# First loads of a linear-attention block kernel moved between two DMA queues and cut smaller, with three filler matmuls and a split last store

## The chip, the cores and the metric

The kernel runs on one core of a Trainium2 chip. The metric is device time in microseconds; lower is better. Executions of one kernel mostly agree within 0.3%. A profile is one execution taken by the hardware profiler; its times count from the start of its span, which is about 1.26 us shorter than the device time. Engines are PE (TensorE matmul), PEld (its weight loads), DVE (VectorE), ACT (ScalarE), POOL and SP. SP and ACT also issue DMA transfers: "sync queue" is SP's, "scalar queue" ACT's. All runs gave a correct result.

## The reference, cut to what matters

```python
x  = A_x                                   # (1, 2048, 448), bf16
xn = _layernorm(x)
s  = linear_attention(xn, A_wqkv, A_wo)    # 16 heads of 28, phi(t) = (t>0 ? t+1 : exp(t)) + 1e-6
h  = relu(xn @ B_w1 + B_b1) ** 2           # 448 -> 1792
g  = silu(h @ B_w2 + B_b2)
return x + s * g
```

## The kernel before

A small program object collects operations with their reads and writes. A list scheduler orders ACT, DVE and POOL from modelled times; PE and SP keep program order. The 2048 tokens are 16 tiles of 128. The head normalizes tiles 0 to 3 on DVE and ACT, transposes them on PE, and starts the k projection (k0, k1) and the first hidden units (H0 to H3).

The loads, in the order in which each queue issues them:

```python
load_x(0, 1)                               # tile 0, sync
load_x(1, 2, "act").prio = -118            # tile 1, scalar queue
load_k("sp", w_qkv, A_wqkv, "wk", 384, 2 * D)   # 384 rows in one transfer, then two 64-row tails
load_x(2, 4, "act").prio = -117            # tiles 2, 3, scalar queue
dma("act", b1r[0:NF, :], ...).prio = -115  # b1, scalar queue
load_w1("w1a", 0, 512, 2)                  # two 384-row parts, then two 64-row tails
load_x(4, 8)                               # tiles 4 to 7, 448 KB
load_w1("w1b", 512, 1024)
load_k("sp", w_qkv, A_wqkv, "wq", 0, 384)
load_w1("w1c", 1024, F)
# ... (later loads cut)
```

The head on PE, and what follows it on DVE:

```python
warm(10, wide=True)                        # ten 512-column fillers on a constant
# ...
turn(0, 0, "act")                          # two transposes of tile 0, evicted by ACT
turn(0, 1, "act")
turn(1, 0, "act")
mains(k0, (0, 1), [("xT", 0, 0)] + wnames("wk")[:1])
turn(1, 1, "dve")
mains(k0, (2,), [("xT", 0, 1)])
k_mains(k1, 1)
# ... (H0 to H3, tiles 2 and 3 cut)
rests(k0, k1)
k0.out()       # phi: exp on ACT, then two operations on DVE that free the PSUM bank
k1.out()
```

The scheduler put the statistics of tiles 4 and 5 on DVE ahead of the phi operations of k0 and k1. DVE works in this order, so a late tile 4 holds up phi, phi holds PSUM banks, and PE's fourth group of products (H4, H6) needs those banks.

The last tile is stored once, after both column parts are done:

```python
full(ss(15, ca, eng="dve", end=False), KS, ["msz"])
full(gg(15, cb, True), range(NF + 1))
full(ss(15, cb, eng="dve", end=False), KS, ["msz"])
store(15, [ca, cb], "act")
```

## Time and profile before

| | before |
|---|---|
| device time, first 3 runs | 142.25 us median (142.16 to 142.40) |
| span of the profiled run | 141.2 us |
| first transpose, first k matmul on PE | 5.26, 6.16 us |
| tiles 4 to 7: issued, landed, used by DVE | 5.31, 9.23, 10.07 us |
| last store: issued, landed | 139.45, 141.17 us |

The page of the kernel before, busy microseconds with their share of the span, and from its part on the chain that ended last the shares by engine:

```profile
PE 137.8 (98%) x1225; PEld 68.4 (48%) x1225; DVE 92.0 (65%) x224; ACT 78.7 (56%) x152; POOL 22.9 (16%) x38
...
PE 98%; DVE 0%; issue 0%; DVEq 0%
```

PE is the limit nearly everywhere. A time lost on PE anywhere is lost at the end, and a wait elsewhere costs nothing until PE waits for it.

The timeline of DVE of the kernel before (start, duration, engine, line, operation, output and inputs):

```profile
9.73 0.42 DVE L513 COPY xT<-pb 128x512 bf16<-128x512 bf16 x1 [0.32 <-PE pb L503]
10.07 1.14 DVE L451 BATCH_NORM_STATS2 st<-x_tok 128x6 f32<-128x448 bf16 x2
11.13 0.67 DVE L595 TENSOR_SCALAR qk<-qk 128x512 bf16<-128x512 bf16 x2
11.71 1.28 DVE L602 SCALAR_TENSOR_TENSOR qk<-pb,qk 128x512 bf16<-128x512 f32 x2
```

The statistics of tiles 4 and 5 (10.07 us) stand ahead of the phi of k (11.13 and 11.71 us), and start without a wait: their data has been there for 0.84 us (10.07 - 9.23).

The table by stage of the kernel before: stretch in us, busy time and number of instructions of PE, PEld, DVE, ACT, POOL, then the granted PE clock, the mean busy share of the 16 DMA engines, and GB/s:

```profile
3.00:4.00 1.00, 1.00 (x4) 0.37 (x3) 0.60 (x1) 0.00 (x0) 0.64 (x3) 1.00 0.95 311
...
8.00:9.00 1.00, 1.00 (x13) 0.79 (x11) 0.85 (x4) 0.65 (x3) 0.00 (x0) 1.00 1.00 366
...
12.00:14.00 2.00, 2.00 (x22) 0.91 (x20) 2.00 (x6) 1.97 (x6) 0.00 (x0) 1.00 0.69 241
```

The DMA engines move over 300 GB/s from 3 to 4 and from 8 to 9 us, and PE is busy for all of the stretch from 12 to 14 us.

The end of the kernel before, from the timeline:

```profile
139.16 0.26 DVE L973 TENSOR_TENSOR xn<-xn,x_tok 128x192 bf16<-128x192 bf16 x1
139.45 0.37 ACTq L396 DMA_DIRECT2D out_dram<-xn  x1
```

The landing records of this store end at 141.17 us: it takes 1.72 us from issue to landing.

### The profile page before, as it was taken

The page shows a single profiled execution, that of the slowest core. Times are in us where ns is not written, and L with a number is a line of the kernel's source. Part 1 is how long each engine was busy: PE and PEld are TensorE (multiplying, and loading weights), DVE is VectorE, ACT ScalarE, POOL GpSimd, SP SyncE. Part 2 cuts the span into 40 slices and gives each one's busy share as a digit, 9 for nine tenths or more (in the row PEclk, how much of TensorE's full clock was granted, in tenths as well). Part 3 has the DMA queues.
Part 4 walks back from the last instruction along what each step waited for, and adds up shares of the span by engine and source line. Part 5 has one row for each costly group of instructions (what it writes and reads, how often), then busy time and mean ns, then how long its engine had stood idle before and what let it go on. Part 6 is the DMA issues. An engine that isn't in the chain of part 4 may idle for free.

```text
span 141.2 us, 3056 instructions
## 1 busy us (share of the span) xinstructions
PE 137.8 (98%) x1225; PEld 68.4 (48%) x1225; DVE 92.0 (65%) x224; ACT 78.7 (56%) x152; POOL 22.9 (16%) x38
## 2 busy tenths in 40 slices
PE   7999999999999999999999999999999999999992
PEld 2366444444444444444445445654555555555482
DVE  0989978898878998779959910127936062452743
ACT  3558787987888897879799571333033030300220
POOL 6000000000000000000680000000001419092670
DMA  4997266999713400000000025880000202122032
GB/s 111 310 312 235 50 170 97 366 300 210 137 23 74 84 14 0 0 9 14 0 0 0 5 76 151 200 155 14 5 0 0 68 2 89 41 66 69 33 102 67
DMA packets 20210, 12.91 MB, mean 91 GB/s; under 512 B 9380, under 2 KB 19812, under 8 KB 20196
## 3 DMA queue, kind: packets, MB, share of 16 engines
q1 hardware_dynamic: 18044, 11.22, 32.1%
q10 hardware_dynamic: 2152, 1.50, 4.4%
q8 instruction: 10, 0.16, 0.5%
q14 instruction: 4, 0.03, 0.1%
HBM read 8.78 MB, written 2.10 MB: 77 GB/s over the span
## 4 chain that ended last, share of the span: by engine, by line
PE 98%; DVE 0%; issue 0%; DVEq 0%
PE pb L928 30%; PE pb L661 30%; PE pb L614 9%; PE pb L994 8%; PE pb L695 7%; PE pb L645 6%; PE pb L1035 3%; PE pb L503 1%; PE pb L701 1%; PE pb L788 1%; PE pb L749 1%; PE pb L826 0%; DVE xn L964 0%; PE pb L819 0%; DVE xn L973 0%; PE pb L784 0%
## 5 line engine op out<-in xcount | busy, mean ns | idle before, releaser
L661 PE MATMUL pb<-xT,w 64*128 64x512 bf16 (+2 forms) x408 | 51.3, 365 | 0.0
L928 PE MATMUL pb<-w,r 64*128 64x448 bf16 (+3 forms) x378 | 44.7, 343 | 0.0
L670 ACT ACTIVATE r<-pb,b1f 128x512 bf16<-128x512 f32 x56 | 35.0, 690 | 2.8 <-PE pb L661 2.8
L661 PEld LDWEIGHTS pb<-xT,w 64*128 64x128 bf16 (+1 forms) x408 | 22.8, 94 | 22.1 <-ACT r L670 0.5
L928 PEld LDWEIGHTS pb<-w,r 64*128 64x128 bf16 (+1 forms) x378 | 22.8, 95 | 20.0 <-issue 1.2
L904 ACT ACTIVATE gbuf<-gbuf 128x448 bf16<-128x448 bf16 (+1 forms) x16 | 8.6, 564 | 36.4 <-DVE gbuf L939 34.3
L939 DVE TENSOR_TENSOR gbuf<-pb,b2b 128x448 bf16<-128x448 f32 (+1 forms) x16 | 9.3, 608 | 29.3 <-PE pb L928 29.3
L973 POOL TENSOR_TENSOR xn<-xn,x_tok 128x448 bf16<-128x448 bf16 x15 | 15.0, 1030 | 48.8 <-DVE xn L964 48.8
L614 PE MATMUL pb<-w_qkv,xT 64*128 64x512 bf16 (+1 forms) x106 | 17.9, 379 | 0.0
L645 PE MATMUL pb<-xT,w_qkv 64*128 64x512 bf16 x84 | 15.5, 376 | 0.0
L678 DVE TENSOR_TENSOR r<-r 128x512 bf16<-128x512 bf16 x39 | 13.5, 416 | 0.0
L385 POOL MEMSET kvm<- 128x2048 bf16 x1 | 1.8, 1804 | 64.4 <-DVE zb L639 64.4
L451 DVE BATCH_NORM_STATS2 st<-x_tok 128x6 f32<-128x448 bf16 x16 | 9.3, 611 | 3.4 <-DMA x_tok<-in_A_x_dram 3.4
L592 ACT ACTIVATE qk<-pb 128x512 bf16<-128x512 f32 x16 | 8.9, 594 | 4.1 <-PE pb L614 3.6
L602 DVE SCALAR_TENSOR_TENSOR qk<-pb,qk 128x512 bf16<-128x512 f32 x16 | 10.7, 686 | 0.3
L994 PE MATMUL pb<-msb,pqT 64*128 64x448 bf16 (+3 forms) x93 | 10.9, 343 | 0.0
L964 DVE TENSOR_TENSOR xn<-pb,gbuf 128x448 bf16<-128x448 f32 (+2 forms) x17 | 9.2, 590 | 2.0 <-ACT gbuf L904 1.5
L679 ACT ACTIVATE r<-r 128x512 bf16<-128x512 bf16 x17 | 9.7, 651 | 0.0
L614 PEld LDWEIGHTS pb<-w_qkv,xT 64*128 64x128 bf16 (+1 forms) x106 | 6.7, 95 | 6.2 <-DVE xT L513 0.2
L695 PE MATMUL pb<-qk,xn 128*128 128x448 bf16 x48 | 9.4, 352 | 0.0
L592 ACT ACTIVATE pqT<-pb 128x512 bf16<-128x512 f32 x12 | 6.8, 597 | 3.1 <-PE pb L661 1.6
L645 PEld LDWEIGHTS pb<-xT,w_qkv 64*128 64x128 bf16 x84 | 6.0, 94 | 5.0
(77 smaller groups left out, 98.9 us busy)
## 6 DMA issues: line engine op xcount, KB each, us to landing
out_dram<-xn SPq DMA_DIRECT2D x15, 112.0 KB, 1.7
w<-in_B_w_dram SPq DMA_DIRECT2D x1, 1568.0 KB, 9.8
x_tok<-in_A_x_dram SPq DMA_DIRECT2D x3, 448.0 KB, 3.8
xT<-rows ACTq DMA_DIRECT2D x6, 112.0 KB
w<-in_B_w_dram SPq DMA_DIRECT2D x1, 576.0 KB, 5.7
xT<-rows SPq DMA_DIRECT2D x5, 112.0 KB
w_o<-in_A_wo_dram SPq DMA_DIRECT2D x1, 392.0 KB, 11.0
w_qkv<-in_A_wqkv_dram SPq DMA_DIRECT2D x1, 384.0 KB, 4.7
```

The lines of the kernel that those rows point to most:

```text
L592: add("act", lambda e, _: e.activation(out=slot, in_=src(), func=AF.Exp), [buf, "actw"], [tile], 0.6)
L602: lambda e, _: e.scalar_tensor_tensor(out=slot, in0=src(), scalar=1.0 + 1e-6, in1=slot, op0=ALU.add, op1=ALU.max),
L614: return e.matmul(ps(b)[:, 0:512], xT[half[h], c, si * P : (si + 1) * P], w_qkv[half[h], c, 384 : 2 * D], start=start, stop=stop,)
L645: return e.matmul(ps(b)[:, 0:512], w_qkv[half[h], c, m * P : (m + 1) * P], xT[half[h], c, g * 512 : (g + 1) * 512], start=start, stop=stop,)
L661: return e.matmul(ps(b)[:, c0 : c0 + n], w_1[half[h], c, fi * P : (fi + 1) * P], xT[half[h], c, t : t + n], start=start, stop=stop,)
L670: lambda e, _: e.activation(out=slot, in_=ps(b)[:, 0:512], func=AF.Relu, bias=b1f[:, fi : fi + 1]),
L678: return e.tensor_tensor(out=slot, in0=slot, in1=slot, op=ALU.mult)
L679: return e.activation(out=slot, in_=slot, func=AF.Square)
L695: last = e.matmul(ps(b)[:, 0:D], xn[:, si, c * P : (c + 1) * P], pk_of(si), start=(si == 0), stop=(si == NT - 1),)
L928: return e.matmul(ps(b)[:, 0:n], r2[half[h], fi, si * P : (si + 1) * P], w_2[half[h], fi, c], start=start, stop=stop)
L973: eng, lambda e, _: e.tensor_tensor(out=ob, in0=ob, in1=x_tok[:, si, c], op=ALU.add),
L994: return e.matmul(ps(b)[:, 0:n], q, m, start=start, stop=stop)
```

## The change

Its intent: get tile 0 without competition from tile 1, let the k product start on its first row chunk, keep PE busy between the first transposes, and leave a smaller store for the end. The diff, cut to its core:

```diff
         load_x(0, 1)
-        load_x(1, 2, "act").prio = -118
-        load_k("sp", w_qkv, A_wqkv, "wk", 384, 2 * D)
-        load_x(2, 4, "act").prio = -117
-        dma("act", b1r[0:NF, :], ...).prio = -115
+        dma("act", b1r[0:NF, :], ...).prio = -118
+        load_x(1, 2)
+        load_x(2, 4, "act").prio = -116
+        for c in range(3):
+            dma("sp", w_qkv[:, c, 384 : 2 * D], A_wqkv[c * P : (c + 1) * P, 384 : 2 * D],
+                [("wk", (0, 3, 4)[c])], P * 1024)
+        for i in (0, 1):
+            dma("sp", w_qkv[half[i], 3, 384 : 2 * D], A_wqkv[384:448, 384 : 2 * D], [("wk", 1 + i)], 64 * 1024)
@@
         turn(0, 1, "act")
+        warm(3)
         turn(1, 0, "act")
-        mains(k0, (0, 1), [("xT", 0, 0)] + wnames("wk")[:1])
+        mains(k0, (0,), [("xT", 0, 0), ("wk", 0)])
+        mains(k0, (1,), [("wk", 3)])
         turn(1, 1, "dve")
-        mains(k0, (2,), [("xT", 0, 1)])
+        mains(k0, (2,), [("xT", 0, 1), ("wk", 4)])
@@
         full(ss(15, ca, eng="dve", end=False), KS, ["msz"])
+        store(15, ca)
         full(gg(15, cb, True), range(NF + 1))
         full(ss(15, cb, eng="dve", end=False), KS, ["msz"])
-        store(15, [ca, cb], "act")
+        store(15, cb, "act")
```

(`store` now takes one column range; cut.)

More of the change, by code (lines that the diff above doesn't have):

```diff
@@ L389, in late_constants @@
             pool(lambda e, _: e.memset(msz[:, :, :], 0.0), ["msz"], gate, dur=0.85)
+        half = (slice(0, 64), slice(64, 128), slice(0, 128))
         x_r = A_x[0].rearrange("(p s) d -> p s d", s=NT)
@@ L425, in bass_recurrent_scan__linear_attn_block__dense_activation_squared_relu__prompt_kernel @@
         w1_of = lambda fi: "w1a" if fi < 4 else "w1b" if fi < 8 else "w1c"
-        wnames = lambda name: [(name, i) for i in range(4 if name == "w1a" else 3)]
+        wnames = lambda name: [(name, i) for i in range({"w1a": 4, "wk": 5}.get(name, 3))]
         table = add("act", lambda e, _: e.preload_act_table_set("natural_log_exp_and_others"), [], ["actw"], 0.1)
@@ L429, in bass_recurrent_scan__linear_attn_block__dense_activation_squared_relu__prompt_kernel @@
         load_x(0, 1)
-        load_x(1, 2, "act").prio = -118
-        load_k("sp", w_qkv, A_wqkv, "wk", 384, 2 * D)
-        load_x(2, 4, "act").prio = -117
-        dma("act", b1r[0:NF, :], B_b1.rearrange("(f p) -> f p", p=P), ["b1r"], F * 2, ["b1r"]).prio = -115
+        dma("act", b1r[0:NF, :], B_b1.rearrange("(f p) -> f p", p=P), ["b1r"], F * 2, ["b1r"]).prio = -118
+        load_x(1, 2)
+        load_x(2, 4, "act").prio = -116
+        for c in range(3):
+            dma(
+                "sp", w_qkv[:, c, 384 : 2 * D], A_wqkv[c * P : (c + 1) * P, 384 : 2 * D], [("wk", (0, 3, 4)[c])],
+                P * 1024,
+            )
+        for i in (0, 1):
+            dma("sp", w_qkv[half[i], 3, 384 : 2 * D], A_wqkv[384:448, 384 : 2 * D], [("wk", 1 + i)], 64 * 1024)
         load_w1("w1a", 0, 512, 2)
@@ L527, in bass_recurrent_scan__linear_attn_block__dense_activation_squared_relu__prompt_kernel @@
         MM = lambda n: n / 2400 + 0.003
-        half = (slice(0, 64), slice(64, 128), slice(0, 128))
         def phase(lo, hi):
@@ L975, in residual, with store @@
             )
-        def store(si, parts, eng="sp"):
+        def store(si, c=slice(0, D), eng="sp"):
             dma(
-                eng, o_r[:, si, :], obuf[:, si % 8, :], [("out", si)], P * D * 2,
-                [("o", si % 8, c.start) for c in parts],
+                eng, o_r[:, si, c], obuf[:, si % 8, c], [("out", si, c.start)], P * (c.stop - c.start) * 2,
+                [("o", si % 8, c.start)],
             )
@@ L999, in out @@
                 if end:
-                    store(si, [slice(0, D)])
+                    store(si)
             return Acc(b, reads_s(si), mm, out, n)
@@ L1048, in k_mains @@
         def k_mains(u, si):
-            mains(u, (0, 1), [("xT", si, 0)] + wnames("wk")[:1])
+            mains(u, (0, 1), [("xT", si, 0)])
             mains(u, (2,), [("xT", si, 1)])
```

## The prediction

> **What bounds the kernel now.** TensorE. The page has PE busy 137.8 of 141.2 us and 98% of the chain that ended last. The chain shows PE work without a visible break from 5.26 us to about 138.7 us. After that come 0.37 + 0.26 us of DVE and the last store, issued at 139.45 us and landed at 141.17 us. The change can therefore win only before about 10.2 us, where the scheduled stream becomes dense, or after 138.7 us.
>
> **The head before** (timeline and landings, us from the span's start). Ten filler matmuls run from 0.84 us, started 0.427 us apart, and end near 5.06. x tile 0 lands at 3.38, tile 1 at 3.57. DVE starts statistics at 3.40 and is almost never idle until the last transposed tile at 10.15. The first transpose starts at 5.25 (DVE releases it), the first k matmul at 6.16. All three row chunks of the k weights land together at 5.99, the evicted transpose is ready at 6.07, and PE is itself busy until 6.156: three limits nearly equal. The k matmuls start 0.43 us apart until about 6.67, then 0.215. The Trainium skill ("TensorE: Matmul & The Clock Gate", "The HAM clock gate") gives a clock that doubles after a busy window of about 3.4 us whose phase is free; this trace agrees in the factor 2, and the switch came 5.8 us after the first matmul.
>
> **What the change does.**
> 1. Tile 0 no longer shares the DMA engines with tile 1. Its 128 packets of 41 ns were spread over 1.0 us; I estimate a landing 0.2 us earlier. Tile 1, second on sync, should land near 3.6, still before DVE wants it (about 3.95). The DVE head starts about 0.2 us earlier, the first transpose at about 5.06.
> 2. Three narrow fillers at 0.107 us (a quarter of 0.427) add 0.32 us of PE before tile 1's transpose, where PE idled only about 0.15 us. With step 1 this puts the first k matmul at about 6.16 again: a wash. It gains up to 0.2 us only if the clock has risen earlier.
> 3. Row chunks take the k weights off the list of limits (first chunk near 5.0), but the limit beside it stays.
> 4. Three more issues on sync (0.4 to 0.6 us each) shift all later loads: w1, tiles 4 to 7 by about 1 us. Tiles 4 to 7 landed at 9.23 and DVE takes them at 10.07, so DVE may wait 0.2 to 0.4 us; w1's first part (7.04, needed 7.82) has just enough slack.
> 5. The last store shrinks from 896 to 384 bytes a row. Its first packet starts 0.87 us after issue, data takes 0.47 us, completion 0.37 us. Only the middle shrinks: 512-byte packets took 34 ns against 41 for 896, so I estimate 0.1 us saved. The skill ("DMA: Bandwidth & Descriptors", "Specifications") warns of a read-modify-write below 512 bytes; no trace here shows such a store.
>
> **Sum.** Head 0 (-0.3 to +0.3), tail -0.1, and a little less scatter from the k weights: **142.05 us**, 8 in 10 between 141.6 and 142.4. Faster by over 2%: 0.01; within 2%: 0.98; slower: 0.01.
>
> **What would show it.** Tile 0 landing near 3.2, first transpose near 5.06, first k matmul still 6.1 to 6.2, tiles 4 to 7 landing near 10.2, last store 1.6 instead of 1.72 us, PE 98% of the chain.
>
> **What would make it wrong.** The clock rising earlier or later than at 6.67 (up to 0.4 us either way); tile 1 landing after 4.1, which delays all of DVE; a late tile 4 delaying DVE's eviction of k and so PE's free banks near 12.8 us; the list scheduler, given other issue times, ordering later DVE and ScalarE work differently.

## The result, and the profile after

| | before | after |
|---|---|---|
| device time, 6 runs each | 142.30 us median (142.16 to 142.47) | 142.59 us median (142.33 to 143.19) |
| span of the profiled run | 141.2 us | 141.9 us |

The ratio is 1.0027, 95% interval 1.0005 to 1.005. Ratios here are the mean time of one kernel's fast runs over the mean of the other's fast runs of the same rounds, so not quite the ratio of the quoted medians. Executions over 1.5% slower than the fastest of the same kernel are left out of the means. The change is slower by about a quarter of a percent, and its runs scatter over 0.86 us where those of before scatter over 0.31. The profiled run is the slowest of the six, so its losses are larger than typical.

The instruction order of DVE is unchanged by the change, and PE has the three fillers more. The scheduler, which the prediction feared, reordered nothing.

The page of the kernel after, the same parts:

```profile
PE 137.9 (97%) x1228; PEld 69.2 (49%) x1228; DVE 92.0 (65%) x224; ACT 78.7 (55%) x152; POOL 22.9 (16%) x38
...
PE 89%; SPq 4%; DMA 3%; DVE 2%; issue 1%; DVEq 0%
```

PE's busy time is equal, but the chain is no longer all PE: it starts on the sync queue and passes through a DMA transfer. The chain that ended last of the kernel after, in order of time (start, duration, what):

```profile
6.03 0.04 issue
6.07 0.60 SPq L397
6.67 0.04 issue
6.71 4.72 DMA x_tok<-in_A_x_dram
11.43 0.02 issue
11.45 1.15 DVE st L458 x2
12.61 0.40 DVE qk L601 x2
13.00 0.61 DVE qk L608
13.61 0.05 issue
13.66 1.04 PE pb L667 x8
```

Read it downwards: the sync queue reaches the load of tiles 4 to 7 only at 6.71 us, the load lands at 11.43, DVE's statistics waited for it, phi of k waited for the statistics, and PE's next group waited for phi's banks. Matched one by one with those of before, PE's matmuls are 0.06 us ahead just before this group and 0.88 us behind from it to the end. A second load was late as well: the last part of w1b landed at 13.17 us (11.03 before), so with phi in time this group would still have stood until about then, instead of starting near 12.73.

The waits of the kernel after between 10 and 15 us (who waited for whom, us in total, times, longest); the same view of the kernel before has neither the first nor the last line:

```profile
DVE st L458 <- DMA x_tok<-in_A_x_dram: 1.4, 1, 1.4
PEld pb L667 <- DVE qk L608: 1.3, 1, 1.3
...
PE pb L667 <- DVE qk L608: 0.8, 1, 0.8
```

The timeline of DVE of the kernel after, to be laid against that of before:

```profile
9.66 0.42 DVE L520 COPY xT<-pb 128x512 bf16<-128x512 bf16 x1 [0.33 <-PE pb L510]
11.45 1.15 DVE L458 BATCH_NORM_STATS2 st<-x_tok 128x6 f32<-128x448 bf16 x2 [1.36 <-DMA x_tok<-in_A_x_dram]
12.52 0.48 DVE L601 TENSOR_SCALAR qk<-qk 128x512 bf16<-128x512 bf16 x2
```

The table by stage of the kernel after:

```profile
3.00:4.00 1.00, 1.00 (x4) 0.37 (x3) 0.97 (x3) 0.16 (x1) 0.64 (x3) 1.00 0.64 184
...
8.00:9.00 1.00, 0.99 (x11) 0.92 (x12) 0.86 (x4) 0.66 (x3) 0.00 (x0) 1.00 0.74 153
...
12.00:14.00 2.00, 1.23 (x14) 0.41 (x10) 2.00 (x6) 1.58 (x3) 0.00 (x0) 1.00 0.97 258
```

PE loses 0.77 us between 12 and 14 us. Earlier, the DMA engines moved 184 GB/s where they had moved 311, and 153 where they had moved 366, at a lower busy share (0.64 and 0.74). Only the first of the two differences will turn out to follow the cause: from 8 to 9 us before_chunks, which loses nothing, moved 276 GB/s, and before_tile1_sync, which loses 0.9 us, 333 (both kernels are described below).

The timeline of PE of the kernel after, in the head:

```profile
5.06 0.63 PE L510 MATMUL pb<-ident,xn 128*128 128x128 bf16 x4
5.49 0.53 PE L1041 MATMUL pb<-const-bfloat16-1.0 128*128 128x128 bf16 x3
5.80 0.42 PE L510 MATMUL pb<-ident,xn 128*128 128x128 bf16 x2
6.02 0.92 PE L620 MATMUL pb<-w_qkv,xT 128*128 128x512 bf16 x2
```

Tile 0 landed at 2.94 us instead of 3.38, the first transpose starts 0.20 us earlier and the first k matmul 0.14 us earlier; by the last products of k (9.95 us before, 9.88 after) the gain is 0.07 us. In the tail, the last store takes 1.56 us instead of 1.72.

So this profile adds up as follows. The head gives 0.07 us. The last matmul starts 0.88 us later (138.415 before, 139.296 after), so 0.95 us was lost in between, nearly all of it at the wait above. The tail gives 0.16 us back. The sum is +0.72 us (0.88 - 0.16), against +0.7 us in the spans.

### The profile page after: what moved, and what is told of

Same layout as the page of the kernel before. It is cut to its first block, busy times and chain, and to the rows that moved or that the text cites. A ratio compares the mean times of both kernels' runs of the same rounds, so it can differ in the third digit from the quotient of the medians.

```text
span 141.9 us, 3067 instructions
## 1 busy us (share of the span) xinstructions
PE 137.9 (97%) x1228; PEld 69.2 (49%) x1228; DVE 92.0 (65%) x224; ACT 78.7 (55%) x152; POOL 22.9 (16%) x38
## 4 chain that ended last, share of the span: by engine, by line
PE 89%; SPq 4%; DMA 3%; DVE 2%; issue 1%; DVEq 0%
PE pb L934 30%; PE pb L667 28%; PE pb L1000 8%; PE pb L620 7%; PE pb L701 6%; PE pb L651 6%; SPq L397 4%; DMA x_tok<-in_A_x_dram 3%; PE pb L707 1%; DVE st L458 1%; PE pb L794 1%; PE pb L755 1%; PE pb L832 0%; DVE qk L608 0%; DVE qk L601 0%
```

## The experiments

Kernels are compared only within the same rounds. All outputs are right. Medians of before in the later calls were 142.29 to 142.34 us. Eighteen kernels ran, all timed in five rounds: twelve on the first theory and its repairs, four on the order of the first loads, two on what was left.

**First theory:** three more issues on sync push the load of tiles 4 to 7 out of DVE's slack. **Rivals:** the fillers, the row chunks, the split store.

### The split store alone

Kernel before, with `store(15, ca)` moved forward and `store(15, cb, "act")` last, as in the change.

> The kernel before, with only the last tile's store cut in two (512-byte rows early on sync, 384-byte rows last on the scalar queue). Theory (late tiles 4 to 7 cost the time, the tail pays): about 0.16 us faster than before, ratio near 0.999, because the profile after showed 1.56 us from issue to landing of the last store against 1.72. Rival (the small-row store is what costs): slower than before by 0.2 us or more.

Measured: 142.43 us median (142.16 to 142.66), ratio 1.0010 (0.9998 to 1.0022). Neither the gain nor the loss. The packet and landing records of the last store show why the gain is small. In four profiles with the whole store (before, before_dve_swap, before_x47_late, swap_one_store) issue to landing took 1.72 us each. In six profiles with the split one (after, dve_swap, x47_before_tails, k_one, tail_only, no_warm) it took 1.56, 1.56, 1.55, 1.68, 1.72 and 1.74. A 384-byte packet took 22 ns against 44 to 45 for 896 bytes, so the data phase did shrink, from 0.49 to between 0.31 and 0.41 us. But completion after the last data took 0.34 to 0.38 us in the good half and 0.46 to 0.53 us in the others. The six split stores profiled later took 1.54 to 1.91 us; over all twelve the mean is 1.69, only 0.03 below the 1.72 of the six undisturbed whole ones. Two whole ones, in kernels described below, took 2.34 and 2.37.

### DVE reordering

The changed kernel; after scheduling, the four phi operations of k0 and k1 on DVE go ahead of the statistics of tiles 4 and 5:

```diff
         pr.schedule()
+        dve = pr.order["dve"]
+        sts = [o for o in dve if o.writes[0] in (("st", 4), ("st", 5))]
+        phis = sorted((o for o in early if o.eng == "dve"), key=dve.index)
+        # ... put phis ahead of sts, give sts start times behind them
         pr.emit(nc, es)
```

> The changed kernel, with one reordering on DVE: the four phi operations of k tiles 0 and 1 come before the statistics of x tiles 4 and 5, so that a late load of tiles 4 to 7 no longer holds them up. Nothing else moves. Theory: the PE wait on DVE's phi (0.8 us in the profile after) disappears, the median falls by 0.4 to 0.5 us to about 142.05 to 142.15, and the scatter of runs shrinks from 0.9 us to about 0.3. Rivals (three filler matmuls, row chunks, or split store as the cause): no change, 142.6 and the same scatter.

Measured: 142.08 us median (141.74 to 142.35), ratio 0.9983 (0.9971 to 0.9996). The median fell by 0.5 us against the changed kernel, as the theory asked, and the profile has no PE wait after the start. This supports that the loss goes through DVE's wait for tiles 4 to 7. It does not show why these are late. In this profile they landed at 10.39 us. The rule found below (landing plus 127.87) would have put the last matmul at 138.26 in the old DVE order; it started at 137.97, so by this estimate the reordering saved 0.29 us here. The rest is the head: of the 0.45 us by which it leads the profile of before, 0.41 is there at the second k matmul already (6.17 us against 6.58), as the clock had risen at 5.4 us instead of 6.7.

### Tiles 4 to 7 earlier on sync

```diff
-        load_w1("w1a", 0, 512, 2)
-        load_x(4, 8)
+        load_w1("w1a", 0, 512, 2, lambda: load_x(4, 8))   # ahead of its two 64-row tails
# ... (the new argument of load_w1 cut)
```

> The changed kernel, with the load of x tiles 4 to 7 issued two places earlier on sync, ahead of the two 64-row tails of the first w1 part. Theory: its issue moves from 6.7 to about 5.6 us and its landing to about 9.2 to 10.4, within DVE's slack, so most of the loss goes (142.1 to 142.3), unless the tails, now behind 448 KB, land after 9.9 and hold PE by up to 0.3 us. Rivals: no change.

A miss: 142.86 us (142.60 to 143.08), ratio 1.0040. The tiles landed at 10.25, but the tails behind them at 10.45 and 10.65, and PE wanted those at 9.6. The waits of this kernel on PE:

```profile
PE pb L667 <- DMA w<-in_B_w_dram: 0.8, 1, 0.8
```

The wait moved to the transfer that had been overtaken.

### Without the fillers

`warm(3)` removed from the changed kernel.

> The changed kernel without the three narrow filler matmuls. Theory: the fillers cost at most 0.05 us, because the k matmuls were held by the evicted transpose and the low clock anyway: median still about 142.5, same scatter, the PE wait on DVE's phi still there. Rival (fillers push the k matmuls and all that follows): faster by 0.2 us or more. Second rival (fillers keep the clock from rising late): slower by 0.2 or more.

Measured: 142.80 us (142.19 to 143.57), ratio 1.0032 (1.0007 to 1.0058). No gain from leaving the fillers out, and none lost beyond the scatter: the profile has the same DVE wait (1.3 us, tiles landing at 11.02). PE's own wait of 0.7 us stands there under an ACT operation that ended at 13.20 us, its weight load's under DVE's phi, which ended at 13.19; the table further down speaks for phi. The clock rose at about 5.8 us here and 6.7 with the fillers. In other profiles with fillers it rose before 4.6 us and at 5.4 (x47_before_tails, dve_swap), and in two with the PE order of before before 4.5 and at 6.67 (tail_only, before). So its moment varies, and no effect of the fillers on it is visible. The medians without fillers are 0.2 us higher here (142.80 against 142.59) and in a second pair below (143.50 against 143.30), less than the scatter.

### The k weights in one transfer again

```diff
-        for c in range(3): dma("sp", w_qkv[:, c, 384 : 2 * D], ...)
-        for i in (0, 1): dma("sp", w_qkv[half[i], 3, 384 : 2 * D], ...)
+        load_k("sp", w_qkv, A_wqkv, "wk", 384, 2 * D)
# ... (the names that the k matmuls wait for cut)
```

> The changed kernel, with the first 384 rows of the k weights in one transfer again instead of three; order of queues, fillers and split store stay. Two issues fewer on sync (about 0.95 us), so tiles 4 to 7 are issued near 5.8 us and land near 9.5 to 10.5. Theory (their landing sets the time once it is later than about 10.1 to 10.5): most runs no longer wait, median 142.1 to 142.3, scatter smaller. Rival (moving tile 1 to sync or the fillers cost the time): still 142.5 or more.

A miss, and the first blow to the theory: 142.88 us (142.41 to 143.78), ratio 1.0040. Issued at 5.75 us, the tiles landed between 8.94 (first of 16 engines) and 11.90 us (last). The k weights were late too (6.58 us), and PE waited 0.9 us for them.

### Tiles 4 to 7 late in the kernel before

The kernel before; only on SP's list, the load of tiles 4 to 7 goes behind the three transfers of w1b:

```diff
         pr.schedule()
+        sp = pr.order["sp"]
+        i = next(i for i, o in enumerate(sp) if o.writes[0] == ("x", 4))
+        sp[i : i + 4] = sp[i + 1 : i + 4] + [sp[i]]
         pr.emit(nc, es)
```

> The kernel before, with one thing moved: the load of x tiles 4 to 7 is issued after the three transfers of the second w1 part, 1.6 us later; the order of every compute engine is unchanged. Theory: it lands near 11.0 to 11.5 us, DVE waits 0.9 to 1.3 us, PE loses what exceeds its slack of about 0.4 us, and the last matmul starts about 127.9 us after the landing, as in the changed kernel and in the run without fillers: 142.7 to 143.2, with the wider scatter of the changed kernel. Rival (lateness of this load is harmless): 142.3.

Measured: 143.43 to 144.86 us in four fast runs, and two runs at 146.5 and 146.7; ratio of the fast ones 1.0138 (1.0112 to 1.0164). One late load alone costs more than the whole change. The profile, which is the fastest of the six, has it landing at 11.52 us, DVE waiting 1.4 us and PE 0.8. Why the other runs are up to 3 us longer was not seen; they have no profile.

### The DVE reordering with the whole store, and on the kernel before

First: the reordering on the changed kernel, with the store of before.

> The run with the DVE reordering, but with the last tile's store whole again (896-byte rows), so the split is judged with the rest of the change in place. If the split saves the 0.1 us of the prediction: 142.2, slower than the reordering with the split (142.08). If it saves nothing, as the run of the split alone suggests (142.43 against 142.30): 142.0 to 142.1.

Measured: 142.30 us median (141.95 to 143.34), ratio 1.0005 (0.9982 to 1.0028). The interval is too wide to price the store. The profiled run is the slow one, and it shows a second load out of its slack: tiles 4 to 7 landed at 11.13 us and cost nothing, but the last part of w1b landed at 13.05, where PE wanted it at 12.27, and PE stood until 13.25. The view of waits puts this under an ACT operation that ended at 13.13. But in dve_swap the same group of matmuls started at 12.34, while that ACT operation ended only at 13.20, so w1b is the likelier cause. In the kernel before w1b had landed by 11.03 us.

Second: the reordering on the kernel before.

> The kernel before with the DVE reordering alone. Theory (the reordering only removes a wait that exists when the load is late): no change, 142.2 to 142.4, since tiles 4 to 7 landed there at 9.2 us, before DVE asks. Rival (evicting k earlier is a gain of its own): faster by 0.2 us or more.

Measured: 142.53 us (142.31 to 143.22), ratio 1.0019 (1.0003 to 1.0036). No gain, as the theory said; a small loss it did not foresee and which stays unexplained. In its profile one of the 16 DMA engines landed its share of tiles 4 to 7 at 10.50 us, the other fifteen by 8.96, so a late single engine also occurs with the old order of loads.

### The k tails on the scalar queue

The two 64-row tails issued by ACT behind tiles 2 and 3:

```diff
-            dma("sp", w_qkv[half[i], 3, 384 : 2 * D], ...)
+            dma("act", w_qkv[half[i], 3, 384 : 2 * D], ...).prio = -115 + i
```

This gives sync its issue times back. It ran in four forms: as it is, without fillers, with the whole store, and with the DVE reordering.

> The changed kernel, with the two 64-row tails of the k weights issued on the scalar queue behind tiles 2 and 3 (that engine is idle until 3.8 us) instead of on sync. Every later load on sync is issued about 1.2 us earlier, tiles 4 to 7 near 5.5 us as in the kernel before; all engine orders stay. Theory (the later issues make tiles 4 to 7 and the second w1 part miss their slack): landing of tiles 4 to 7 near 9.2 to 10.0, no PE wait on DVE's phi, median 142.0 to 142.2, scatter 0.5 us or less. Rival (single slow transfers, whatever the issue time, set it): still 142.5 or more with runs above 143.

> The same with the three narrow fillers taken out, to see what they are worth when no load is late. Theory: within 0.1 us of the run with fillers, because the clock rose between 4.5 and 6.7 us in the profiles with and without them, and the first k matmul came at 5.95 to 6.02 both ways. Rival (fillers bring the clock up): slower by 0.2 us or more.

> The same with the last tile's store whole again, to price the split where no load is late. From six profiles of the split store (1.55, 1.56, 1.56, 1.68, 1.72, 1.74 us from issue to landing) against 1.72 in all four whole ones, the split saves 0.08 us on average: this run slower by 0 to 0.15 us than with the split.

> Both remedies: k tails on the scalar queue and k's phi on DVE ahead of the statistics of tiles 4 and 5. If tiles 4 to 7 are in time already, the reordering adds nothing: 142.0 to 142.2. If some runs still have them late, it cuts those: smaller scatter and 141.9 to 142.1.

| | median us | ratio (95%) | tiles 4 to 7 issued; landed, first to last engine |
|---|---|---|---|
| ktails_act | 143.30 | 1.0065 (1.0051 to 1.0080) | 5.42; 8.93 to 10.99 |
| ktails_act_nowarm | 143.50 | 1.0098 (1.0066 to 1.0130) | 5.44; 9.08 to 11.25 |
| ktails_act_one_store | 142.81 | 1.0040 (1.0028 to 1.0053) | 5.42; 9.38 to 10.38 |
| ktails_act_swap | 142.98 | 1.0043 (1.0027 to 1.0060) | 5.41; 9.13 to 11.11 |

All four missed, and the first theory fell in its first half. With the issue at 5.42 us, 0.1 us from that of before, the tiles still landed 1.2 to 2.0 us later, spread over 1.0 to 2.2 us (0.54 before), and the medians were above that of the change itself. The number of issues on sync can't be the main reason. In ktails_act_swap PE also waited 0.4 us for the k weights, which no order of DVE helps. These runs can't price fillers and store either, since the loads swamp both.

The second half of the theory held. In every profile where DVE waited for tiles 4 to 7 long enough to stop PE, the last matmul of the kernel started the same time after their landing (issue times and landings from the DMA records, matmul starts from the trace, us):

| kernel | issued | landed, first to last engine | last matmul starts | minus landing |
|---|---|---|---|---|
| after | 6.71 | 9.78 to 11.43 | 139.30 | 127.87 |
| no_warm | 6.71 | 10.06 to 11.02 | 138.89 | 127.87 |
| k_one | 5.75 | 8.94 to 11.90 | 139.77 | 127.87 |
| before_x47_late | 7.12 | 10.51 to 11.52 | 139.39 | 127.87 |
| ktails_act | 5.42 | 8.93 to 10.99 | 138.86 | 127.87 |
| ktails_act_nowarm | 5.44 | 9.08 to 11.25 | 139.11 | 127.86 |
| before (no wait) | 5.31 | 8.69 to 9.23 | 138.41 | 129.18 |

All these kernels have the DVE order of before. So the slack has a number: with a head like that of before, the landing sets the time once it is later than about 10.5 us (138.41 - 127.87). before_tile1_sync, run later, gives 127.87 again (139.37 - 11.50).

### New suspect: which queue carries tile 1

The packet records pointed at the first loads. In the ten profiles taken so far with the new queue order, 8 to 12 of the 128 packets of tiles 2 and 3 took over 400 ns (median 74), and 378 to 435 KB (of 1000 bytes) had been started by 4 us. In the four with the old order it was 0 or 1 packet, and 521 to 587 KB. The old order has slow packets too, elsewhere: counting all loads up to 5 us, before has 7 and after 11. All slow kernels but two of the old order (before_x47_late, slow on purpose, and before_dve_swap) have the new order of the first loads, also those with fewer issues; but so has dve_swap, the fastest. Four runs take it apart from the number of issues.

The kernel before with only the queue order of the change:

```diff
         load_x(0, 1)
-        load_x(1, 2, "act").prio = -118
+        dma("act", b1r[0:NF, :], ...).prio = -118
+        load_x(1, 2)
         load_k("sp", w_qkv, A_wqkv, "wk", 384, 2 * D)
-        load_x(2, 4, "act").prio = -117
-        dma("act", b1r[0:NF, :], ...).prio = -115
+        load_x(2, 4, "act").prio = -116
```

> The kernel before with only the queue order of the change: tile 1 second on sync, b1 first and tiles 2, 3 second on the scalar queue. One more issue on sync (0.46 us). Theory Q (the order itself makes the early loads slow and uneven): 8 or more packets of tiles 2, 3 over 400 ns, about 400 KB started by 4 us, tiles 4 to 7 landing in a spread of 1 us or more and after 10 us, time 142.5 to 143. Theory I (number of issues on sync): tiles 4 to 7 land 0.5 us later than before, near 9.7, no loss: 142.2 to 142.3.

The same with b1 behind tiles 2 and 3:

> The same, but the scalar queue issues tiles 2, 3 first and b1 last, as the kernel before had b1. If b1 ahead is what slows the load of tiles 2 and 3, slow packets go back to 0 or 1 and the time to 142.3; if moving tile 1 is, it stays as in the run with b1 first.

The changed kernel with the old order (the three scalar-queue lines of before; chunks, fillers and split store stay):

> The changed kernel with the queue order of the kernel before (tile 1, tiles 2 and 3, b1 on the scalar queue); row chunks, fillers and split store stay. Tiles 4 to 7 are issued near 6.25 us. Theory Q: 0 to 1 slow packets, over 520 KB started by 4 us, tiles 4 to 7 landing by about 10.2 with a small spread, median 142.1 to 142.4. Theory I: two issues too many remain of three, landing near 10.2, so about 142.4 with some runs near 143.

The kernel before with only the row chunks:

> The kernel before with only the k weights in row chunks (two more issues on sync, 0.95 us). Both theories put the landing of tiles 4 to 7 near 10.1 to 10.2, at the edge of DVE's slack (10.1 to 10.5): 142.2 to 142.5. Over 142.7 would say that the chunks are a cause of their own.

| | median us | ratio (95%) | packets of tiles 2, 3 over 400 ns | KB started by 4 us | tiles 4 to 7 landed |
|---|---|---|---|---|---|
| before (first profile) | 142.30 | 1 | 0 | 548 | 8.69 to 9.23 |
| before_tile1_sync | 143.25 | 1.0062 (1.0026 to 1.0099) | 9 | 412 | 9.00 to 11.50 |
| before_tile1_sync_b1_last | 142.87 | 1.0028 (1.0009 to 1.0047) | 0 | 588 | 8.77 to 9.64 |
| after_old_queues | 142.25 | 0.9987 (0.9968 to 1.0005) | 1 | 574 | 9.27 to 10.01 |
| before_chunks | 142.28 | 0.9995 (0.9978 to 1.0012) | 1 | 597 | 9.41 to 10.14 |

This settles which part of the change carries the loss. The queue order alone costs 0.9 us in the kernel before (143.25 against 142.34 in the same rounds), and without it the changed kernel is level with before: 142.20, 142.23, 142.25 and 142.32 us. The 0.9 us are uncertain (0.26 to 0.99%), and more than the whole change lost. The order is two moves, tile 1 to sync and b1 ahead, and the first brings one of the change's three extra issues on sync; b1 ahead with tile 1 left on the scalar queue was not run. The row chunks cost nothing, although two more issues bring the tiles' issue to 6.22 us. Their two extra issues stay just inside the slack, while the landings stay close together.

The profile of after_old_queues is of a fifth run, in which the granted clock fell to 0.56 after about 5 us and stayed there; it took 242.9 us. Its DMA records up to the landing above are used with that reservation; before_chunks, with the same queue order and a full clock, agrees with them. The stage from 3 to 4 us by queue order, first before_tile1_sync:

```profile
3.00:4.00 1.00, 1.00 (x4) 0.37 (x3) 0.85 (x3) 0.17 (x1) 0.64 (x3) 1.00 0.63 160
```

then before_chunks:

```profile
3.00:4.00 1.00, 1.00 (x4) 0.36 (x3) 0.63 (x1) 0.00 (x0) 0.64 (x3) 1.00 0.99 334
```

160 and 184 GB/s with tile 1 on sync behind tile 0 and b1 first, 311 and 334 with the old order. Over all profiles it is 122 to 184 in the eleven with the new order, and 263 to 335 in the eight with the old one. Then the wait in before_tile1_sync, first on DVE:

```profile
DVE st L451 <- DMA x_tok<-in_A_x_dram: 1.2, 1, 1.2
```

and on PE:

```profile
PE pb L661 <- DVE qk L602: 0.6, 1, 0.6
PE pb L614 <- ACT xT L514: 0.6, 1, 0.6
```

The first is the wait of the changed kernel, in a kernel that has neither its chunks nor its fillers nor its store. The second stands before the first k matmul (6.59 us against 6.16 before); the view names an ACT operation, and the k weights too landed only at 6.46 us, against 5.99. Together they put the last matmul 0.96 us later than in before (139.37 against 138.41). But this profiled run (144.03 us) is slower than its median, and in it the last store took 2.34 us instead of 1.72, which the loads do not explain: 0.62 of the 1.6 us by which its span is longer lie there.

The variant with b1 last splits the expectation. The slow packets went away, but the time did not return. Tiles 2 and 3 then start at 2.03 us and compete with tiles 0 and 1, which land at 3.63 and 4.35 us instead of 3.38 and 3.57; the first transpose starts at 5.52. But the last matmul starts only 0.21 us later than in before (138.62 against 138.41). Its profiled run, the slowest of its six, had a last store of 2.37 us, and that is 0.65 of the 0.85 us by which its span is longer. So with tile 1 on sync both places of b1 lost; with b1 last, most of what the profile shows is the store, and why the store is longer was not found.

### What is left of the change

The changed kernel with the old queue order, first with the DVE reordering, then with the k tails on the scalar queue.

> The changed kernel with the old queue order and with k's phi on DVE ahead of the statistics of tiles 4 and 5. If the loads decided what was left, runs that still waited for tiles 4 to 7 are gone: 142.0 to 142.25 with a scatter of 0.4 us. If nothing was waiting any more: 142.2 to 142.3, level with the kernel before, and the other two parts (fillers, split store) are worth nothing that can be measured.

> The changed kernel with the old queue order and the two k tails on the scalar queue behind tiles 2 and 3 (ahead of b1). Tiles 4 to 7 are issued near 5.0 us. If the loss in the earlier runs with the tails there came from the queue order of tile 1 and b1, this runs at 142.1 to 142.3 with tiles 4 to 7 landing before 9.7. If putting 128 KB more on the scalar queue is what made the engines uneven, 142.5 or more with a spread of landings over 1 us.

| | median us (range) | ratio (95%) |
|---|---|---|
| before in the same rounds | 142.31 (142.26 to 143.52) | |
| old_queues_swap | 142.24 (142.10 to 142.50) | 0.9978 (0.9948 to 1.0008) |
| old_queues_tails_act | 142.47 (142.22 to 143.06) | 1.0000 (0.9965 to 1.0035) |

Two runs of before took 143.31 and 143.52 us, which lowers both ratios; the medians are the better guide. old_queues_swap is level with before; its median is 0.07 us lower, within the noise. In the second run b1 was issued ahead of the tails, not behind them as the expectation says. Its tiles 4 to 7 were issued at 5.19 us and landed from 8.73 to 10.00 us, a spread of 1.27 us, without a PE wait in the profile. So the expectation fell between its two cases: 0.8 us better than with the tails there in the new queue order, but not better than leaving the tails on sync.

Only dve_swap (142.08 us, ratio 0.9983) of the eighteen kernels had an interval below 1, and the run that differs from it by the whole store did not repeat that. No version is shown to beat the kernel before by more than the runs can resolve.

## Why the prediction was wrong

**TensorE as the bound, and a win only before about 10.2 us or after 138.7 us.** True for winning. The losing lay in between, at 12.7 us, by a wait that begins before.

**Step 1, tile 0 earlier.** Right in direction, with a gain twice as large: landed at 2.94 us (0.2 earlier was estimated, 0.44 came), tile 1 at 3.54 (near 3.6 was said), first transpose at 5.06 as said. The step looked only at these two tiles. What the same move did to the next loads was not asked.

**Step 2, fillers a wash.** Right as far as could be measured: first k matmul at 6.02, the head as a whole 0.07 us better, and no gain from leaving them out. Alone in the kernel before they were not run.

**Step 3, row chunks off the list of limits.** Right, though the first chunk came at 5.41 us and not near 5.0. Alone in the kernel before they measured 142.28 against 142.34.

**Step 4, later loads shifted.** This is the step that failed, in two terms. It said that three more issues "shift all later loads: w1, tiles 4 to 7 by about 1 us", the tiles landing near 10.2, and that "DVE may wait 0.2 to 0.4 us". Measured: issue 1.40 us later, landing 2.20 us later, DVE wait 1.36 us, PE wait 0.8 us. The issue shift was mis-sized: three issues at the 0.47 us that one took here are 1.40, and the prediction's own 0.4 to 0.6 us each already give 1.2 to 1.8. The other 0.8 us (2.20 - 1.40) was not in the sum at all. With the old queue order the landing follows the issue: in before_chunks both came 0.91 us later. With the new order it fell further behind: in before_tile1_sync the issue came 0.44 us later and the landing 2.27. So the runs trace this term to the queue order. An estimate from these numbers: three issues alone would have put the landing at 10.6 us (9.23 + 1.40), 0.1 past the slack. The Trainium skill ("DMA: Bandwidth & Descriptors", "Issuing engines are not separate DMA queues") says that issuing on several engines only saves the sequencer's issue time. By that sentence, moving tile 1 to the other queue costs the later loads one issue there; the prediction reckoned with nothing else for them. Here the bytes were equal and the order, with its one more issue on sync, cost 0.9 us, while two more issues without it (before_chunks) cost nothing.

**Step 5, the tail.** Right for the profile of the change (0.16 us), too high on the whole: 0.1 us was estimated, the twelve split stores took between 0.18 us less and 0.19 us more than 1.72, 0.03 less on the mean. The data phase shrank as said, the completion, taken as fixed, grew in most. Alone the split could not be told from zero.

**The sum** put the head at 0 and the wait of DVE at 0, though the list of what would make it wrong named "a late tile 4 delaying DVE's eviction of k and so PE's free banks near 12.8 us". That chain was the loss. The error was to call DVE's slack enough without asking how far the landing scatters: the last engine of a load came up to 3.0 us behind the first (k_one), and one engine is enough.

**Open.** Why the packets of tiles 2 and 3 are slow when tile 1 goes on sync and b1 first is not known. The records show that they are slow, and that starting tiles 2 and 3 earlier (b1 last) makes them fast and tiles 0 and 1 late. The link from these packets to the scatter of the later landings is a common appearance in the profiles, not a tested step, and two profiles go against it: dve_swap has 10 slow packets and a spread of 0.42 us, before_dve_swap 1 slow packet and a spread of 1.88. Open too is why the last store took 2.34 and 2.37 us in the two kernels before with tile 1 on sync, so how much of their loss the loads account for in a typical run.

## What to carry to other kernels

When a change reorders the first loads, follow every later load to its first reader and compare its landing, with its scatter, to the moment it is needed; here two loads that nobody had touched were the ones that hurt. An in-order engine that does early work for later tiles ahead of work that frees PSUM turns a late load into a PE stall, so try putting what frees buffers first where data may be late; here it helped the changed kernel (142.08 us) and not the kernel before (142.53). Test the parts of a bundled change alone: one of its four parts cost 0.9 us, two could not be told from zero, and the fillers were only ever tested by leaving them out.

## What the Trainium skill lacked or had wrong

- "DMA: Bandwidth & Descriptors", "Issuing engines are not separate DMA queues": the section treats the choice of the issuing engine as a matter of issue time alone. With equal bytes, moving one tile from the scalar to the sync queue and b1 ahead went with 160 GB/s instead of 311 from 3 to 4 us and with 143.25 us instead of 142.34.
- The same page has no figure for how far the engines of one transfer finish apart: 0.42 to 2.96 us between first and last of 16 for the 448 KB load of tiles 4 to 7. It is the last that the reader waits for.
- The same page, "Specifications", names 512 bytes as the least size for full rate. The 384-byte store packets took 22 ns against 44 for 896 bytes, so 17 bytes per ns against 20, a small loss; what varied was completion, 0.34 to 0.67 us over the twelve split stores.
- "TensorE: Matmul & The Clock Gate", "The HAM clock gate", says that the moment at which the clock rises varies by 500 ns either way. Here it varied more: from about 3.7 us (swap_one_store) to 6.7 us (before, after), that is 2.9 to 5.8 us after the first matmul.
- The same section has a caveat on a clock seen stuck at a quarter for over 50 us. One run here had a granted clock of 0.56 from about 5 us to the end, some 236 us (device time 242.9 us); what set it off is unknown.
